# Loading q and k of six batches with the two heads of a pair side by side

## The chip, the core and the metric

The kernel runs on one core of one Trainium2 chip. The metric is device time in microseconds (us) of one execution, from launch to the last store. The core has five instruction queues that matter here: TensorE (PE; its weight loads are listed as PEld), VectorE (DVE), ScalarE (ACT), GpSimd (POOL) and SyncE (SP). Sixteen DMA engines move data between HBM and the on-chip memory; they serve the queues in which POOL, SP and ACT put their transfers.

## The reference

Eight batches of a 12-head attention with squared ReLU in the place of softmax, then a feed-forward layer over all 3584 tokens:

```python
# q, k, v: (batch 8, heads 12, seq 448, head_dim 64), float32
scale = 1.0 / np.sqrt(q.shape[-1])
scores = scale * np.matmul(q, k.transpose(0, 1, 3, 2))
attn = np.maximum(scores, 0.0) ** 2 / S          # S = 448
attn_out = np.matmul(attn, v)
# tokens side by side, heads joined: x is (3584, 768)
x = attn_out.transpose(0, 2, 1, 3).reshape(B * S, H * D)
h = x @ w_in                                     # w_in: (768, 2048)
g = 0.5 * h * (1.0 + erf(h * inv_sqrt2))         # exact GELU
return g @ w_out                                 # w_out: (2048, 768)
```

## The kernel before

**Stages.** Attention works on one batch `b` and one group `g` of four heads at a time (`G = 3` groups). The keys of a group are cut into seven blocks of 64 (`NK = 7`). A step (`add_steps`) is one block against all 448 queries for the four heads: TensorE makes the scores in 64-row tiles, two heads on the lower and two on the upper half of the partitions (L749); ACT or DVE scales them and takes the ReLU (L761, L763); DVE squares them (L770). After seven steps, `add_av` multiplies the squares by v (L810), and two copies bring the result to `xT`, the transposed input of the feed-forward layer. The first layer of that is plain for batches 0 to 4 (`add_f1`, L862, GELU in L872); for the last three batches it is cut in blocks and done with seven products in the place of eight on sums of the blocks (`add_wsums`, `add_blocks`, L1006, L1043), as is the second layer for all 14 groups of 256 tokens (`add_group`, L1179, L1213). All matmuls are bf16, and the loads of q, k, v and the weights convert from float32 on their way (POOL's queue).

**Transposed q and k.** The scores need q and k with the head dimension on the partitions (`qT`, `kT`). For batches 0 and 1 TensorE transposes them (`add_tk`, `add_tq`). For batches 2 to 7 a DMA of SP's queue does (`add_T_dma`, L660): it takes 128 columns of the loaded `nq` or `nk` at a time and lays them on 128 partitions. `nk` holds 7 column blocks of 64 for heads 0 and 1 of the group (one head on each half of the partitions), then 7 for heads 2 and 3; `nq` holds 4 column blocks for each of the four heads. The scores want heads 0 and 1 on the lower half of `qT` and `kT` and heads 2 and 3 on the upper, but a turned block of 128 columns has two blocks of the *same* head above each other (in the seventh of a group's k, one of each). The kernel before solves that in two ways. For k, the loop of the scores goes over the blocks in the order in which they lie, and the index of the square is worked out with `divmod` in `add_av`. For q, one turn per group fills every second slot of `qT` (`slots_of`), from a source that begins 64 columns into `nq` (which is two blocks of 64 longer, and zero in these), and `fill_halves` copies each half to the other half of the neighbouring slot: two copies for a group, by DVE or ACT. In `fn_qk` the moving operand is then picked by a slot number `n`.

**Order of the work.** The functions `add_...` only describe operations: which engines can do each and what it waits for. The list `ORDER` says which operation comes next on which engine: `P` is TensorE, `A` ACT, `D` DVE, `G` POOL, `S` SP, and the number is that of the operation in the order of creation; the class `Scheduler` merely places the operations by that list (`place`), and instructions run in that order on each engine. All gate and load numbers of POOL are in this list too.

**Loads.** POOL issues all loads. `nq` and `nk` have one buffer for all of batches 2 to 7, `qT` and `kT` have two. So loads of batch b+2 wait until batch b+1 is turned: a small POOL operation that reads `qT` of group g (`add_gate`, L709; `add_vgate`, L719) stands ahead of the loads of k and q of group g of the next batch (`add_k`, L546; `load_q`, L467) and holds POOL's queue until the turn has landed. A batch has three loads of k, three of q and one of v. POOL may have eight loads on the way; a load waits for the eighth before it. SP issues the turns (two per group, 36 in all) and the stores.

**Stores.** `store_rows` (L1140) writes 128 rows of the output. The row order of q within a batch is `(p c)` for all batches (query p x 4 + c stands in place c x 112 + p), so a tile of 128 rows is in two pieces of the output, and two DMAs store it; the last group uses SP and ACT for them.

**Buffers at the end.** `wtile` puts sums of `w_in` for the last three batches in buffers that q and k no longer need: `ws1` in that of `nq`, `ws4` in that of `nk`, `ws2` in one of the two of `qT`.

Of the kernel before, what the change touches and what calls it, by code (L numbers as in the profile page):

```python
# [13 lines left out]
KC = 112  # L14
# [10 lines left out]
SLOTS = H * NC + 1  # L25
# [58 lines left out]
A10 D13 G0 G1480 Z1024 P14 P11 D15 G1 G3 G4 G7 G118 G2 D12 A16 P17 P36 A37 G117 G121 G6 D18 P33 D34  # L84
P21 A22 P19 P39 A40 P42 G125 A43 P23 D20 D24 P51 A52 D35 P25 D26 P48 Z672 D41 D38 A49 G126 P63 A64
D50 P57 P66 A67 P31 P27 D32 P102 D65 A58 P108 D103 D28 D44 A109 P111 A112 D68 P29 D30 P54 A55 G5 D53
P69 P131 A70 D59 P45 D132 P96 A97 P90 A91 P129 P133 P81 P93 G8 G122 G120 D104 D46 A47 G124 A82 G119
D71 D134 D130 P72 G128 A94 P137 D56 D138 A73 D74 P75 D110 A76 P139 D83 P105 A106 D113 D107 D140 P60
A61 A62 P84 A85 P78 D98 P168 A79 A169 G123 G9 P141 P174 A175 G127 G239 G238 G241 G147 P114 A115 A116
D86 P162 D95 A163 P135 D92 P99 A100 A101 G148 D77 D80 P87 A88 P204 A89 D136 P198 A205 D170 A142 G150  # L90
D199 P145 A146 P165 D166 P171 D172 D173 P156 A157 D158 P243 A244 P247 A248 P183 G151 A184 P159 P207
D206 G153 G154 P257 D167 D164 A258 D160 D161 S228 S229 P255 A256 P253 A208 P189 A254 P213 A190 D176
P177 S231 D214 P180 A181 D178 P216 P267 D217 A179 G237 A268 P219 A220 D182 P195 S232 S234 P210 P249
D191 G240 D211 A250 D215 P265 A266 D196 D197 P143 P186 S235 P222 D221 G149 G152 G155 D218 A144 P192
D193 A223 P263 A264 P251 A187 D224 A252 P261 A262 P259 A260 D194 D188 D185 D200 P201 A202 D209 D212
P225 A226 D203 P245 A227 A246 P366 A367 P364 A365 P368 A369 P352 A353 D383 D384 P372 A373 P356 A357
D388 D380 D389 D381 D386 P378 A379 P348 A349 G242 G269 G270 G271 G272 D385 G273 G274 P354 A355 P370
D382 P362 A371 D387 P350 A363 A351 P360 D230 P285 A286 P291 A361 P288 A289 P374 A375 S408 P358 P294
D292 P282 A295 D293 A283 P276 P392 D233 P315 D287 D277 P318 D236 A359 D319 A316 P279 A280 A393 P376
P309 A310 P300 D317 A377 A301 D290 P333 P396 D278 D281 D284 D390 D296 D302 P394 D395 D311 S409 S411  # L100
S412 D391 A334 D335 P339 A340 P306 A307 P297 G417 A298 D299 D397 P327 A328 P398 P303 P324 G420 A325
D399 S414 S415 D429 D326 P312 A313 P400 D401 A304 D308 D314 D320 P402 D305 P404 D405 D427 D428 P330
A331 P336 D403 A337 D338 P321 D341 P342 A343 P431 P433 D410 A322 A323 P447 D432 A448 P459 A460 P453
D434 P435 A436 D454 D455 P450 A451 D413 P456 S406 A457 P462 D329 P437 P439 P471 G275 G423 G418 D344
A463 D332 P345 D438 A472 D440 G419 P477 P474 D430 A475 D570 D452 D458 P441 G421 A346 A347 D442 D449
A478 P443 D444 P480 D416 D461 P489 P465 A490 G422 G424 G425 A466 P539 A540 P525 A526 A481 P541 D464
S551 P486 A487 D467 A542 P507 D508 P468 P483 P504 A505 S407 S552 G560 A469 A470 S554 S555 D484 P521
A522 D473 P529 A530 G563 P513 P501 P495 D479 A496 S557 P545 A546 A514 D485 P543 A544 D476 S445 D509
# [50 lines left out]
A1395 A1355 P1425 D1424 A1375 D1426 P1427 D1428 A1389 P1429 A1361 D1433 D1434 P1437 A1438 D1430  # L159
D1435 P1439 D1440 S1431 S1432 D1436 P1441 D1442 P1443 D1444 P1445 D1446 P1447 D1455 P1449 D1448  # L160
D1453 D1454 P1457 D1450 D1456 P1459 D1458 D1460 P1461 P1463 D1462 S1451 S1452 S1473 D1464 P1465
D1466 P1467 D1468 P1470 S1474 P1469 D1471 D1472 S1475 S1476 S1477
"""


# [1355 lines left out]
```

## Time and profile before

| | |
|---|---|
| time, median of 3 runs (lowest to highest) | 365.88 us (365.56 to 365.89) |
| profiled execution: time, span | 365.83 us, 364.1 us |
| granted TensorE clock, mean over the span | 0.999 |
| loads of q in POOL's queue: number, KB, median us to landing | 21 of 224 KB, 8.7 |
| loads of k in POOL's queue | 23 of 224 KB, 8.2 |
| HBM read, written | 45.61 MB, 11.01 MB |

The span runs from the first to the last instruction of the trace; the time of an execution is 1.73 us more here. Times in the views below are in us from the start of the span, unless marked ns. A busy share says how long an engine had an instruction, not whether it was on the path that sets the end; that is read from the chain of waits, which goes back from the last instruction to what released each one. "issue" in such a place means that the engine waited for nothing that the profile shows. The DMA share is the mean busy share of 16 engines, and can go above 1 where it is added up over packets that overlap.

### The profile page before, as it was taken

The page shows a single profiled execution, that of the slowest core. Times are in us where ns is not written, and L with a number is a line of the kernel's source. Part 1 is how long each engine was busy: PE and PEld are TensorE (multiplying, and loading weights), DVE is VectorE, ACT ScalarE, POOL GpSimd, SP SyncE. Part 2 cuts the span into 40 slices and gives each one's busy share as a digit, 9 for nine tenths or more (in the row PEclk, how much of TensorE's full clock was granted, in tenths as well). Part 3 has the DMA queues.
Part 4 walks back from the last instruction along what each step waited for, and adds up shares of the span by engine and source line. Part 5 has one row for each costly group of instructions (what it writes and reads, how often), then busy time and mean ns, then how long its engine had stood idle before and what let it go on. Part 6 is the DMA issues. An engine that isn't in the chain of part 4 may idle for free.

```text
span 364.1 us, 8583 instructions
## 1 busy us (share of the span) xinstructions
PE 355.2 (98%) x3589; PEld 225.4 (62%) x3589; DVE 296.7 (82%) x515; ACT 214.3 (59%) x348; POOL 63.7 (17%) x104
## 2 busy tenths in 40 slices
PE   8889999999999999999999999999999999999995
PEld 3567555445555455454555556889888688867663
DVE  3988989299979998979989999999877775767662
ACT  4987755586777685888887887236353043214400
POOL 8565710431401404215010000000000000000000
PEclk9999999999999999999999999999999999999999
DMA  9999999999999999999795211002002030022223
GB/s 169 198 202 204 202 204 190 164 180 169 185 191 157 156 136 169 211 157 177 142 192 78 88 43 46 2 2 66 24 2 86 2 86 2 2 86 88 87 68 107
DMA packets 72326, 42.97 MB, mean 118 GB/s; under 512 B 37984, under 2 KB 68960, under 8 KB 72288
## 3 DMA queue, kind: packets, MB, share of 16 engines
q0 software_dynamic: 32912, 22.47, 43.9%
q1 hardware_dynamic: 38736, 19.46, 26.1%
q8 instruction: 28, 0.46, 0.5%
q10 hardware_dynamic: 640, 0.51, 0.4%
q14 instruction: 10, 0.08, 0.1%
HBM read 45.61 MB, written 11.01 MB: 156 GB/s over the span
## 4 chain that ended last, share of the span: by engine, by line
PE 90%; DVE 4%; DMA 3%; ACT 1%; issue 1%; DVEq 0%
PE pso L1179 34%; PE psh L862 21%; PE pb L1006 18%; PE ps L749 9%; PE pav L810 8%; DVE a_sq L770 2%; DMA out_dram<-osb 1%; ACT a_sq L761 1%; DMA k<-in_k_dram 1%; PE tp L605 1%; DVE a_sq L763 1%; DVE qT L511 1%; DVE osb L1213 0%; DVE kT L511 0%; DVE s_sb L1160 0%
## 5 line engine op out<-in xcount | busy, mean ns | idle before, releaser
L761 ACT ACTIVATE a_sq<-ps 128x896 bf16<-128x896 f32 (+1 forms) x137 | 120.0, 929 | 27.1 <-PE ps L749 26.8
L770 DVE TENSOR_TENSOR a_sq<-a_sq 128x896 bf16<-128x896 bf16 x169 | 96.9, 616 | 2.7 <-ACT a_sq L761 1.7
L862 PE MATMUL psh<-xT,win_sb 128*128 128x448 bf16 (+1 forms) x420 | 77.0, 337 | 0.0
L1179 PEld LDWEIGHTS <-s_sb 128*128 128x128 bf16 x456 | 43.0, 98 | 29.6 <-issue 4.9
L862 PEld LDWEIGHTS <-win_sb 128*128 128x128 bf16 x420 | 39.2, 98 | 35.3 <-issue 7.0
L1043 DVE TENSOR_TENSOR part<-pb,part 128x448 f32<-128x448 f32 x80 | 47.5, 620 | 16.5 <-PE pb L1006 15.4
L749 PE MATMUL ps<-qT,kT 64*64 64x448 bf16 (+1 forms) x756 | 49.1, 337 | 2.0 <-ACT a_sq L761 0.8
L1179 PEld LDWEIGHTS <-h_sb 128*128 128x128 bf16 x336 | 31.9, 98 | 22.6 <-issue 3.6
L872 ACT ACTIVATE h_sb<-psh 128x448 bf16<-128x448 f32 x64 | 35.2, 553 | 17.1 <-PE psh L862 16.9
L763 DVE TENSOR_SCALAR a_sq<-ps 128x896 bf16<-128x896 f32 x32 | 34.7, 1087 | 9.7 <-PE ps L749 9.4
L1179 PE MATMUL pso<-wout_sb,s_sb 128*128 128x384 bf16 (+2 forms) x232 | 41.1, 321 | 0.0
L1179 PE MATMUL pso<-wout_sb,h_sb 128*128 128x384 bf16 x224 | 41.1, 326 | 0.0
L1179 PE MATMUL pso<-t_sb,s_sb 128*128 128x384 bf16 x224 | 41.0, 326 | 0.0
L1006 PEld LDWEIGHTS <-win_sb 128*128 128x128 bf16 x384 | 36.8, 98 | 2.6 <-issue 0.4
L810 PE MATMUL pav<-a_sq,v_sb 64*64 64x448 bf16 (+1 forms) x756 | 36.2, 329 | 0.0
L749 PEld LDWEIGHTS <-kT 64*64 64x64 bf16 x756 | 19.2, 105 | 23.9 <-issue 18.1
L1213 DVE TENSOR_TENSOR osb<-pso,p_sb 128x384 f32<-128x384 f32 x42 | 23.2, 553 | 10.0 <-PE pso L1179 8.5
L1052 ACT ACTIVATE h_sb<-part 128x448 bf16<-128x448 f32 x48 | 24.4, 574 | 8.0 <-DVE part L1043 8.0
L1006 PEld LDWEIGHTS <-ws 128*128 128x128 bf16 x288 | 27.7, 98 | 1.7
L810 PEld LDWEIGHTS <-v_sb 64*64 64x64 bf16 x756 | 21.3, 107 | 10.8 <-issue 0.6
L513 ACT COPY part<-pb 128x448 f32<-128x448 f32 x16 | 8.1, 529 | 26.6 <-PE pb L1006 26.5
L513 ACT CAST xT<-pav 128x448 bf16<-128x448 f32 (+1 forms) x44 | 20.0, 501 | 5.0 <-PE pav L810 4.9
(61 smaller groups left out, 316.0 us busy)
## 6 DMA issues: line engine op xcount, KB each, us to landing
nk<-in_k_dram POOLq DMA_DIRECT2D x23, 224.0 KB, 8.2
nq<-in_q_dram POOLq DMA_DIRECT2D x21, 224.0 KB, 8.7
v_sb<-in_v_dram POOLq DMA_DIRECT2D x5, 672.0 KB, 8.2
out_dram<-osb SPq DMA_DIRECT2D x7, 336.0 KB, 4.1
v_sb<-in_v_dram POOLq DMA_DIRECT2D x9, 224.0 KB, 8.0
out_dram<-osb SPq DMA_DIRECT2D x7, 288.0 KB, 4.2
out_dram<-osb SPq DMA_DIRECT2D x8, 240.0 KB, 3.1
win_sb<-in_moe_w_in_dram POOLq DMA_DIRECT2D x8, 192.0 KB, 8.5
```

What stands on the lines that cost most here:

```text
L513: A.copy(dst, src)
L749: nc.tensor.matmul(ps[64 * j : 64 * j + 64, e, x * w : x * w + w], kT[r, g, i * 128 + 64 * j : i * 128 + 64 * j + 64], moving, start=True, ...
L761: A.activation(ar, ps, AF.Relu, scale=c_att)
L763: V.tensor_scalar(ar, ps, c_att, 0.0, op0=mybir.AluOpType.mult, op1=mybir.AluOpType.max,)
L770: V.tensor_mul(box["a2"][:, :, :used], ar, ar)
L810: nc.tensor.matmul(pav[0][o2 : o2 + 64, e, :w], vt[b][r, 2 * g + e, bass.ts(i, D)], box["a2"][r, y, o : o + w], start=(i == 0), stop=(i == ...
L862: nc.tensor.matmul(ph[:, x * n : x * n + n], win_sb[:, kd, bass.ts(m + x, 128)], xT[b][:, kd, c], start=(kd == 0), stop=(kd == KD - 1),)
L872: A.activation(h_ring()[:, m : m + nm, o + c.start : o + c.stop], box[0][:, :S].rearrange("p (x n) -> p x n", x=nm), AF.Gelu,)
L1006: nc.tensor.matmul(bank[name][:, y, z * HS : z * HS + HS], w[:, k, bass.ts(mm, 128)], right()[:, k], start=first and k == 0 and z == 0, st ...
L1043: V.tensor_add(get(to), ps(name), get(other))
L1052: A.activation(h_ring()[:, m : m + 2, o + half[c].start : o + half[c].stop], src().rearrange("p (x n) -> p x n", x=2), AF.Gelu,)
L1179: nc.tensor.matmul(box[bank][:, n0:n1], left()[:, kf], right()[:, kf, n0:n1], start=bool(need) and kf == 0, stop=kf == K2 - 1, skip_group_ ...
```

## The change

For batches 2 to 7, `nq` and `nk` are laid out with two heads beside each other: for each group, block after block, 64 columns of head 0 or 1 and 64 of head 2 or 3. A turned block of 128 columns then has one head on the lower 64 partitions and the other on the upper 64, as in batches 0 and 1. To lay them out so, a load of one group is cut in two DMAs (`e`), one for heads 0 and 1 and one for heads 2 and 3, whose pieces are 64 elements wide in the on-chip memory (128 B in bf16). The turns stay, one for k and one for q per group; the copies of `fill_halves` go, and so do the two memsets of the margins of `nq`. `fn_qk` and `add_av` use for all batches the indices that batches 0 and 1 had. `qT` is 112 columns shorter, and `ws2`, which lay in one of its buffers, gets a buffer of its own. The rows of q of batches 2 to 7 are in natural order, so a tile of 128 output rows from batch 2 on is one DMA; in the last group that means SP alone. `ORDER` is new as a whole: the order of the operations on TensorE, ACT, DVE, POOL and SP differs from about 14 us on (the numbers of the operations move as well, since 18 operations are gone).

```diff
-SLOTS = H * NC + 1
...
 ORDER = """
-A10 D13 G0 G1480 Z1024 P14 P11 D15 G1 G3 G4 G7 G118 G2 D12 A16 P17 P36 A37 G117 G121 G6 D18 P33 D34
+A10 D13 G0 G1462 Z1024 P14 P11 D15 G1 G3 G4 G7 G118 G2 D12 A16 P17 P36 A37 G117 G121 G6 D18 P33 D34
...
             elif b == 2:
-                nq[b] = natpool.tile([KC, (H * NC + 2) * D], BF16, tag="nq", name="nq")
-                nk[b] = natpool.tile([128, HP, NK * D], BF16, tag="nk", name="nk")
-                nc.gpsimd.memset(nq[b][:, :D], 0.0)
-                nc.gpsimd.memset(nq[b][:, D + H * NC * D :], 0.0)
+                nq[b] = natpool.tile([KC, G, 2 * NC, 2, D], BF16, tag="nq", name="nq")
+                nk[b] = natpool.tile([128, G, NK, 2, D], BF16, tag="nk", name="nk")
...
     def load_q(b, g0, g1, c0=0, c1=NC):
         get_nat(b)
-        nc.gpsimd.dma_start(
-            q_cols(b)[:, 4 * g0 : 4 * g1, c0 * D : c1 * D], q_view(b, g0, g1, c0, c1)
-        )
+        if b < 2:
+            to = nq[b][:, 4 * g0 : 4 * g1, c0 * D : c1 * D]
+            nc.gpsimd.dma_start(to, q_view(b, g0, g1, c0, c1))
+            return
+        for e in range(2):
+            h = 4 * g0 + 2 * e
+            rows = q[b, h : h + 2].rearrange("j (c p) d -> p (j c) d", p=KC)
+            nc.gpsimd.dma_start(nq[b][:, g0, :, e], rows)
...
-                tpool.tile([128, SLOTS * KC], BF16, tag="qT", name="qT"),
+                tpool.tile([128, HP * S], BF16, tag="qT", name="qT"),
...
     def add_k(b, g0, g1):
         def fn():
             get_nat(b)
-            nc.gpsimd.dma_start(nk[b][:, 2 * g0 : 2 * g1], kv_view(k, b, g0, g1))
-
-        o = dma(fn, (g1 - g0) * 4 * S * 256, war(b, g0, g1))
+            rows = kv_view(k, b, g0, g1)
+            if b < 2:
+                nc.gpsimd.dma_start(nk[b][:, 2 * g0 : 2 * g1], rows)
+                return
+            for e in range(2):
+                nc.gpsimd.dma_start(
+                    nk[b][:, g0, :, e], rows[:, e].rearrange("p (i d) -> p i d", d=D)
+                )
+
+        o = dma(fn, (g1 - g0) * 4 * S * 256, war(b, g0, g1), 1 + (b > 1))
...
-        o = dma(lambda: load_q(b, g0, g1, c0, c1), n, war(b, g0, g1))
+        o = dma(lambda: load_q(b, g0, g1, c0, c1), n, war(b, g0, g1), 1 + (b > 1))
...
-        def slots_of(n, o, k):
+        def q_dst(g):
             return lambda: get_T(b)[0].rearrange("p (s t) -> p s t", t=KC)[
-                :, 2 * n + o : 2 * (n + k) + o - 1 : 2
+                :, 2 * NC * g : 2 * NC * (g + 1)
             ]
 
-        def q_src(n, o, k):
-            return lambda: nq[b][:, 128 * n + D * o : 128 * (n + k) + D * o]
+        def q_src(g):
+            return lambda: nq[b][:, g].rearrange("p s e d -> p (s e d)")
...
         def k_src(g):
-            return lambda: nk[b][:, 2 * g : 2 * g + 2].rearrange("p e f -> p (e f)")
-
-        def fill_halves(g):
...
+            return lambda: nk[b][:, g].rearrange("p i e d -> p (i e d)")
...
-            even = turn(slots_of(8 * g, 1, 8), q_src(8 * g, 1, 8), lands)
-            both = sch.add(
-                (("DVE", 1.0, 1.1), ("ACT", 1.6, 1.7)), fill_halves(g), [even] + old_T(b)
-            )
-            for c, o in enumerate((even, both, both, both)):
-                Tq[b, g, c] = (o, o)
+            op = turn(q_dst(g), q_src(g), lands)
+            for c in range(NC):
+                Tq[b, g, c] = (op, op)
...
-            n = (16 * g + 15) * KC
-            nc.gpsimd.tensor_copy(gate, get_T(b)[0][:, n : n + 16])
+            n = 2 * S * (g + 1)
+            nc.gpsimd.tensor_copy(gate, get_T(b)[0][:, n - 16 : n])
...
-                            if b < 2:
-                                moving = q_rows(b)[r, 2 * g + j, cols(half)]
-                            else:
-                                n = 4 * (4 * g + 2 * ((2 * i + e) // NK) + j) + 1 - e
-                                moving = qT[r, n * KC : n * KC + S]
+                            moving = q_rows(b)[r, 2 * g + j, cols(half)]
...
-                        n, y = (i, e) if b < 2 else divmod(NK * e + i, 2)
-                        _, box, o = SQ[blocks[n]]
+                        _, box, o = SQ[blocks[i]]
...
-                            box["a2"][r, y, o : o + w],
+                            box["a2"][r, e, o : o + w],
...
-                part = tpool.tile([128, SLOTS * KC], BF16, tag="qT", name="ws2")
+                part = wpool.tile([128, 3 * h], BF16, tag="ws2", name="ws2")
...
         queue, j = list(queues or [nc.sync] * 2), 128 * t
+        if j >= 2 * S:
+            queue[-1].dma_start(out[j : j + 128, c], src[:, c])
+            return
         while j < 128 * t + 128:
```

More of the change, by code (lines that the diff above doesn't have):

```diff
@@ L158 @@
[L158 to L162 removed]
+D50 P57 P66 A67 P31 P27 D32 P102 D65 A58 P108 A109 D28 P29 A103 P131 D44 P45 P81 P69 A82 G5 G8 D68
@@ L716, in fn @@
         def fn(e):
-            nc.gpsimd.tensor_copy(gate, get_T(b)[0][:, 31 * KC : 31 * KC + 16])
+            nc.gpsimd.tensor_copy(gate, get_T(b)[0][:, 4 * S - 16 : 4 * S])
         pool_q.append(sch.add((("POOL", 0.2, 0.3),), fn, [Tq[b, 1, 0][0]]))
```

162 lines of the change are left out of this document (77 added, 85 removed).

## The prediction

> **What bounds the kernel now.** I read the page first: how full each engine is, and when.
>
> ```profile
> span 364.1 us, 8583 instructions
> PE 355.2 (98%) x3589; PEld 225.4 (62%) x3589; DVE 296.7 (82%) x515; ACT 214.3 (59%) x348; POOL 63.7 (17%) x104
> PE   8889999999999999999999999999999999999995
> DMA  9999999999999999999795211002002030022223
> q0 software_dynamic: 32912, 22.47, 43.9%
> ```
>
> TensorE is busy 98% of the span; in the first half of the span the DMA engines are never idle either. The table of stages says where TensorE is not busy (columns: stage, its length, then busy time of PE, PEld, DVE, ACT, POOL, granted clock, DMA share, GB/s):
>
> ```profile
> 6.00:32.00 26.00, 22.59 (x575) 16.57 (x572) 22.83 (x44) 22.96 (x37) 16.66 (x25) 1.00 1.34 198
> 32.00:200.00 168.00, 167.90 (x1613) 87.32 (x1614) 146.88 (x244) 124.64 (x188) 42.14 (x70) 1.00 1.14 171
> 200.00:340.00 140.00, 140.00 (x1267) 107.75 (x1264) 113.07 (x202) 63.54 (x120) 0.00 (x0) 1.00 0.14 41
> 340.00:364.10 24.10, 19.99 (x131) 12.24 (x129) 13.15 (x24) 0.69 (x2) 0.00 (x0) 0.98 0.35 99
> ```
>
> Between 32 and 340 us TensorE idles 0.1 us in 308. All slack that a change can win is the 3.4 us of idle time in 6 to 32 us (where ACT and DVE, 88% busy each, set the pace) and the 4.1 us of the tail. In the middle nothing can be won, but much can be lost: the scores of each batch need q and k loaded and turned in time, while DMA works at a share of 1.14. So the question is whether the new loads still arrive.
>
> **The change part by part.** *TensorE.* Both kernels issue the same 3589 matmuls in the same shapes. Four rows of the chain of waits price what the order moves (start, length, line, count):
>
> ```profile
> 74.14 1.41 PE pso L1179 x8
> 127.43 1.30 PE pso L1179 x8
> 114.00 6.92 PE psh L862 x36
> 89.84 1.32 PE pav L810 x28
> ```
>
> The first row is followed by scores in 64-row tiles, the second by other full products: the switch costs 0.11 us. The new order has one switch fewer. Gain 0.1 us.
>
> *The copies between halves* go, 36 of them:
>
> ```profile
> L511 DVE COPY qT<-qT 64x896 bf16<-64x896 bf16 x34 | 14.8, 436 | 4.1 <-DMA qT<-nq 3.3
> L513 ACT COPY qT<-qT 64x896 bf16<-64x896 bf16 x2 | 1.9, 937 | 0.0
> ```
>
> That is 14.8 us of DVE and 1.9 us of ACT, all after 66 us, beside a TensorE that never waits for them: worth the 0.1 us of idle time at most, taken as zero. Were TensorE not full there, a pair would cost 2 x 0.436 = 0.87 us between the landing of a turned q and its scores. That delay is gone, which I count below by comparing landings with scores directly.
>
> *The loads of q and k.* Before, k for four heads is 128 x 2 pieces of 896 B (as written) and q 112 x 4 pieces of 512 B. After, each is two DMAs and 1792 pieces of 128 B. No packet so small is in the trace. The nearest are four stretches, in this order: 8.5 to 9.5 us (all q pieces of 256 B), 13 to 14 us (896 B, with 15 completion words), 98.5 to 102.5 us (mixed loads of an attention batch), 137 to 139 us (transposes alone, 256 B each):
>
> ```profile
> DMA packets 660, 0.17 MB, mean 169 GB/s; under 512 B 660, under 2 KB 660, under 8 KB 660
> DMA packets 237, 0.20 MB, mean 199 GB/s; under 512 B 15, under 2 KB 237, under 8 KB 237
> DMA packets 1280, 0.80 MB, mean 199 GB/s; under 512 B 53, under 2 KB 1280, under 8 KB 1280
> DMA packets 2026, 0.50 MB, mean 251 GB/s; under 512 B 2026, under 2 KB 2026, under 8 KB 2026
> ```
>
> Per engine of 16: 16000/660 = 24.2 ns for 256 B and 16000/222 = 72.1 ns for 896 B, a line of 0.0747 ns/B. It gives 43.3 ns at 512 B. The mixed stretch fits: 64000/1227 = 52.2 ns at a mean of 652 B, line 53.8. Carried on to 128 B it gives 14.6 ns. The transposes, which read 256 B a packet as a new load piece does (f32), take 32000/2026 = 15.8. I take the mean of these two nearest rows, 15.2 ns. The far ends are 9.6 ns (bytes alone) and 24.2 ns (no cheaper than the smallest load packet seen).
>
> A batch's q and k cost 3 x (256 x 72.1 + 448 x 43.3)/16 = 7.1 us of each DMA engine before, and 3 x 3584 x 15.2/16 = 10.2 us after: d = +3.1 us per batch (2.7 at 14.6 ns, 3.5 at 15.8, 9.2 at 24.2, -0.6 at 9.6).
>
> The Trainium skill (DMA: Bandwidth & Descriptors, Specifications) asks 512 B or more for line rate and says that smaller transfers become read-modify-writes. The trace's 256 B packets show no such step; by the rule d would be the 9.2 of a rival below.
>
> *POOL's queue.* 36 issues more. Their time from the load of q:
>
> ```profile
> L467 POOL DMA_DIRECT2D nq<-in_q_dram x24: 727/742/980, 2.4 to 168.2; - x24
> ```
>
> 727 ns is a load of 448 pieces, 980 the one of 1344: 0.28 ns a piece, so 0.85 us for 896. Twelve take 10.2 us where six took 4.4. The pieces of one take 56 x 15.2 = 0.85 us of the engines: issue keeps up, nothing added. Each load also waits for the landing of the eighth before it, which binds only if eight such loads (6.8 us of work) land sooner than they are moved: zero. Two memsets of 0.17 us go. The gates and loads of v stay in place, behind later loads.
>
> *When loads must be there.* The gates on POOL run when a group's q is turned (below: the first q of batches 2, 3, 4 and 5, then the third of 5); the next loads are issued behind the last gate:
>
> ```profile
> 66.51 0.42 POOL L709 COPY gate<-qT 128x16 bf16<-128x16 bf16 x1 [12.77 <-DMA qT<-nq]
> 86.85 0.20 POOL L709 COPY gate<-qT 128x16 bf16<-128x16 bf16 x1 [10.50 <-DMA qT<-nq]
> 109.71 0.20 POOL L709 COPY gate<-qT 128x16 bf16<-128x16 bf16 x1 [13.64 <-DMA qT<-nq]
> 137.59 0.20 POOL L709 COPY gate<-qT 128x16 bf16<-128x16 bf16 x1 [11.12 <-DMA qT<-nq]
> 142.12 0.40 POOL L709 COPY gate<-qT 128x16 bf16<-128x16 bf16 x1 [1.50 <-DMA qT<-nq]
> ...
> 122.17 0.70 POOL L546 DMA_DIRECT2D nk<-in_k_dram  x1 [0.34 <-issue]
> 142.66 0.70 POOL L546 DMA_DIRECT2D nk<-in_k_dram  x1
> ```
>
> And the first scores of batches 2 to 7 on TensorE:
>
> ```profile
> 70.31 0.76 PE L749 MATMUL ps<-qT,kT 64*64 64x448 bf16 x12
> 93.99 0.95 PE L749 MATMUL ps<-qT,kT 64*64 64x448 bf16 x12
> 122.57 0.55 PE L749 MATMUL ps<-qT,kT 64*64 64x448 bf16 x8
> 150.80 0.55 PE L749 MATMUL ps<-qT,kT 64*64 64x448 bf16 x8
> 175.84 0.60 PE L749 MATMUL ps<-qT,kT 64*64 64x448 bf16 x8
> 199.67 0.36 PE L749 MATMUL ps<-qT,kT 64*64 64x448 bf16 x4
> ```
>
> The new TensorE order puts less or more before them: 8 matmuls of the second layer less (batch 3), 12 of the first less (4), one AV block less (5), 6 of the first more (6). By the four rows above that is -1.30, -12 x 0.192 = -2.3, -1.32 and +1.15 us. So the scores are wanted at 70.3, 92.7, 120.3, 149.5, 177.0 and 199.7. Loads of a batch go out only when the last q of the batch before is turned, so delays add up: the n-th batch from 2 is late by n x d against its gate. With d = 3.1: 69.6, 93.1, 119.0, 150.0. Batch 6 is today held by the scores of 4, not by its loads; a load phase of 137.59 - 122.17 = 15.4 us from 142.66 would end at 158.1, plus 5d = 173.6. Batch 7 follows at 158.1 + 4.5 (third q turned after the first) + 0.5 + 15.4 + 6d = 197.1. Batch 3 is late by 0.4 and batch 5 by 0.5. The delay is the largest of these, not the sum: +0.5 us. What is queued behind the waiting scores is all of TensorE's order, so it goes straight into the end. At d = 2.7 nothing is late.
>
> *SP's queue.* Turning itself keeps its 36 DMAs; stores of batches from 2 on are one DMA instead of two, 22 fewer. SP waits for its inputs anyway:
>
> ```profile
> SPq L660 <- DMA nk<-in_k_dram: 99.0, 6, 56.8
> ```
>
> So its shorter queue is worth zero.
>
> *Start and tail.* The order changes from about 14 us on. One gap stands out:
>
> ```profile
> 21.36 0.25 PE L605 MATMUL tp<-ident,nk 128*64 128x128 bf16 x2 [1.10 <-issue]
> ```
>
> It lies in the last turn of k of batch 1, which waited there for nothing that the profile shows; the new order has that turn 16 score matmuls later, and the gap may go (-1.1) or move. Against it, the first product now stands behind one score step more, that is one ReLU on one of two engines:
>
> ```profile
> L761 ACT ACTIVATE a_sq<-ps 128x896 bf16<-128x896 f32 (+1 forms) x137 | 120.0, 929 | 27.1 <-PE ps L749 26.8
> ```
>
> Half of 929 ns, +0.5. I take zero, ends -1.1 and +0.5. The last stores use SP alone, two of 128 rows, where SP and ACT shared them:
>
> ```profile
> 359.30 2.00 SPq L1140 DMA_DIRECT2D out_dram<-osb  x4
> 360.49 0.85 ACTq L1140 DMA_DIRECT2D out_dram<-osb  x2
> ```
>
> 0.5 or 0.43 us an issue, and both halves were issued at the same time: zero, +-0.3.
>
> Sum, against this execution's 365.83 us (the median of the runs is 365.88, 0.05 more): -0.1 + 0.5 = **366.2 us**.
>
> **The rivals.** *Loads starve the scores.* If the price in the crowded stage is 15.8 ns, batch 5 (the worst) is late by 137.59 + 4 x 3.54 - 149.48 = 2.3 us: 368.0. Past d = 2.9 the slope is steep, four to six us per us of d: at d = 5 batch 7 is late by 178.5 + 30 - 199.7 = 8.8: 374.5. For it: the DMA share is above 1 in this stage already. Against it: issue at 0.85 us keeps the load queue short, which lets turns pass sooner. *Each small piece moves its bytes twice*, 14.6 + 9.6 = 24.2 ns: batch 7 is late by 178.5 + 6 x 9.2 - 199.7 = 34 us: about 400. Against it: the 256 B packets lie on the line. (It is what the Trainium skill's rule, named above, would do here.) *The loads are hidden, and the start gains*: d at 2.7 or below and the gap of 1.10 us gone, 365.83 - 0.1 - 1.1 = 364.6, faster; it decides if the price is under 15 ns and no other gap opens. For it: at 14.6 ns every batch still has slack, 0.4 us at the least (batch 3). Against it: the same ACT and DVE work still paces the start.
>
> **How the numbers follow.** Just in time, as forecast: 0.46, own range 365.0 to 367.2. Starved: 0.28, middle 370. Double price: 0.06. Hidden with a gain at the start: 0.20. A measurement here tells about 0.2%, 0.73 us, from no change. Faster by that: 0.18 of the last case and 0.10 of the first, 0.28; within: 0.20 and 0.02, 0.22; slower: 0.16 + 0.28 + 0.06 = 0.50. The range runs from 364.4 (gain at the start, a little more) to 374.6 (d = 5), leaving out the double price and the outer parts of two cases.
>
> **What would show it.** Load packets of 128 B, about 84,000 in the load queue, some 3 us more load work per batch; gates of batches 2 to 5 at about 69.6, 93, 119, 150; no qT<-qT copies; TensorE idle between 32 and 200 us under 1 us, with any wait at the first scores of batches 3 and 5 and put down to the DMA of qT. A price under 14 ns, or loads whose waits overlap with turns, leaves no wait; more than 16 ns shows waits that grow from batch to batch. The start is right if the idle time of TensorE in 6 to 32 us stays near 3.4.

## The result: faster when the loads arrive, and they do not always

The changed kernel took 364.09 us in the median of four executions (363.45 to 364.39), the kernel before 365.86 (365.56 to 365.89): a ratio of 0.9954, 95% interval 0.9941 to 0.9966. That is 1.8 us less, where 366.2 was forecast, and 0.3 us below the range. Two later series of twelve executions each, on two chips, came out otherwise: medians of 366.07 (363.68 to 371.42; ratio 1.0015, 0.9985 to 1.0046) and 365.79 (363.72 to 369.25; ratio 1.0002, 0.9976 to 1.0028). The kernel before, in executions beside these, had medians of 365.4 and 365.6. In four of the series below the slowest execution (371.42, 369.25, 369.90 and 372.96 us) counts as slow; the ratios leave it out, and no conclusion rests on it. Both results have to be explained: a gain of 1.8 us, and its loss in about half of the later executions. Of these 24 only seven lie at or below 364.4, as all of the first four do; why the first four were all so fast stays open.

The page of the changed kernel, in an execution of 363.45 us:

```profile
span 361.6 us, 8548 instructions
PE 353.9 (98%) x3589; PEld 224.5 (62%) x3589; DVE 287.1 (79%) x487; ACT 209.2 (58%) x340; POOL 105.9 (29%) x138
PE   8889999999999999999999999999999999999995
DMA  9999999999999999999999711002001120202222
q0 software_dynamic: 85328, 22.47, 65.9%
```

The load queue has 85,328 packets for the same 22.47 MB, and its share of the engines grew from 43.9% to 65.9%. POOL's busy time went from 63.7 to 105.9 us. Yet TensorE's row looks as before. The stages (columns as in the prediction's table of stages):

```profile
6.00:32.00 26.00, 23.13 (x572) 17.04 (x570) 23.76 (x45) 24.01 (x38) 17.26 (x26) 1.00 1.36 200
32.00:200.00 168.00, 168.00 (x1619) 86.59 (x1618) 139.31 (x221) 120.21 (x184) 83.74 (x103) 1.00 1.62 167
200.00:340.00 140.00, 140.00 (x1259) 108.14 (x1258) 110.85 (x198) 62.47 (x116) 0.00 (x0) 1.00 0.14 46
340.00:361.60 21.60, 17.96 (x119) 11.01 (x117) 12.30 (x23) 0.00 (x0) 0.00 (x0) 1.00 0.29 108
```

By busy time TensorE gained 0.1 us between 32 and 200 us. That reading is wrong, and the forecast rested on it. A matmul that is pipelined counts as busy to its modelled end: one of the scores is listed with 0.35 us, though the next step can follow 0.19 us after its start. So most of a wait of 0.3 us between two steps of scores vanishes under it. So I counted otherwise: each matmul gets the time by which matmuls of its kind follow each other when nothing is in the way (0.189 us for 448 columns, in proportion for others; four 64-row tiles side by side count as one), and at a given amount of finished work the time lost so far is the clock minus that sum. The changes between tile sizes are in it; the changed kernel has one fewer, worth 0.1 us by the prediction's rows. Time lost in each stage, from the starts of all 3589 matmuls, in us (the stages end at the work that the kernel before has finished at 13 and at 31 us):

| profiled execution | up to 13 us (same code) | 13 to 31 us | 31 us to the last matmul's start | from there to the end of the span |
|---|---|---|---|---|
| before | 4.99 | 3.79 | 13.26 | 4.34 |
| changed | 4.45 | 3.20 | 12.36 | 3.89 |
| changed, third series | 5.04 | 3.40 | 14.35 | 3.89 |

The span is 2.5 us shorter: 0.5 ahead of any change, 0.6 in the start, 0.9 in the middle, 0.4 to 0.5 in the tail. The 0.5 ahead of the change is one execution against another. The chain of waits shows it at the first transposes, of before and then of the changed kernel (start, length, line, count):

```profile
5.81 0.43 PE tp L605 x8
```

```profile
5.24 0.43 PE tp L607 x8
```

Other executions of either kernel began between these two or later. This is most of why 2.5 us of span are 1.8 us of medians.

Where the 0.9 us of the middle was hidden, the order in time of before shows (start, length, engine, line). Twelve matmuls of three score steps take 0.76 us when nothing is late:

```profile
145.26 0.76 PE L749 MATMUL ps<-qT,kT 64*64 64x448 bf16 x12
152.69 1.06 PE L749 MATMUL ps<-qT,kT 64*64 64x448 bf16 x12
...
152.03 1.08 DVE L763 TENSOR_SCALAR a_sq<-ps 128x896 bf16<-128x896 f32 x1
```

The second step at 152.69 needed the buffer of an earlier step, whose ReLU DVE began only at 152.03 and ended 0.4 us after the scores had begun. The prediction itself quotes such a row, 0.95 us for twelve at 93.99, and did not read it; there the trace names one of the copies in `qT` as what came last. Before, 20 of 24 such groups take 0.76 or 0.77 us and four take 0.90, 0.95, 0.96 and 1.06, some 0.8 us too much in all; in the changed kernel all 21 that stand in one row take 0.76. The Trainium skill (Perfetto Trace Analysis, Identifying the Most-Contended Engine) says that matmul occupancy is no good measure of how close TensorE is to its limit, because matmuls are pipelined. This trace agrees: 0.1 us of idle time, and some 0.8 us of waits in four groups of the same stretch.

### The profile page after: what moved, and what is told of

Same layout as the page of the kernel before. It is cut to its first block, busy times and chain, and to the rows that moved or that the text cites. A ratio compares the mean times of both kernels' runs of the same rounds, so it can differ in the third digit from the quotient of the medians.

```text
span 361.6 us, 8548 instructions
## 1 busy us (share of the span) xinstructions
PE 353.9 (98%) x3589; PEld 224.5 (62%) x3589; DVE 287.1 (79%) x487; ACT 209.2 (58%) x340; POOL 105.9 (29%) x138
## 3 DMA queue, kind: packets, MB, share of 16 engines
q0 software_dynamic: 85328, 22.47, 65.9%
## 4 chain that ended last, share of the span: by engine, by line
PE 94%; ACT 4%; DMA 1%; DVE 0%; issue 0%; DVEq 0%
PE pso L1164 36%; PE psh L844 21%; PE pb L988 18%; PE ps L732 10%; PE pav L792 9%; ACT a_sq L744 3%; DMA k<-in_k_dram 1%; PE tp L607 0%; PE tp L635 0%; ACT xT L508 0%; DVE nk L506 0%; DVE kT L506 0%; DVE osb L1198 0%; ACT qT L508 0%; DVEq L1501 0%
## 5 line engine op out<-in xcount | busy, mean ns | idle before, releaser
L744 ACT ACTIVATE a_sq<-ps 128x896 bf16<-128x896 f32 (+1 forms) x132 | 115.0, 923 | 26.0 <-PE ps L732 25.6
L746 DVE TENSOR_SCALAR a_sq<-ps 128x896 bf16<-128x896 f32 x37 | 40.3, 1088 | 13.0 <-PE ps L732 12.8
L732 PE MATMUL ps<-qT,kT 64*64 64x448 bf16 (+1 forms) x756 | 47.7, 336 | 1.5 <-ACT a_sq L744 0.7
L1034 ACT ACTIVATE h_sb<-part 128x448 bf16<-128x448 f32 x48 | 25.5, 577 | 26.8 <-DVE part L1025 26.8
L546 POOL DMA_DIRECT2D nk<-in_k_dram x36 | 34.7, 968 | 9.0 <-DMA wout_sb<-in_moe_w_out_dram 7.8
L732 PEld LDWEIGHTS <-kT 64*64 64x64 bf16 x756 | 18.3, 105 | 22.7 <-issue 17.0
L464 POOL DMA_DIRECT2D nq<-in_q_dram x36 | 30.0, 837 | 2.3 <-DMA wout_sb<-in_moe_w_out_dram 2.1
```

The costliest lines, as they stand in the source:

```text
L464: nc.gpsimd.dma_start(nq[b][:, g0, :, e], rows)
L546: nc.gpsimd.dma_start(nk[b][:, g0, :, e], rows[:, e].rearrange("p (i d) -> p i d", d=D))
L732: nc.tensor.matmul(ps[64 * j : 64 * j + 64, e, x * w : x * w + w], kT[r, g, i * 128 + 64 * j : i * 128 + 64 * j + 64], moving, start=True, ...
L744: A.activation(ar, ps, AF.Relu, scale=c_att)
L746: V.tensor_scalar(ar, ps, c_att, 0.0, op0=mybir.AluOpType.mult, op1=mybir.AluOpType.max,)
```

## The experiments

### The parts one by one, and old and new crossed

**Old order for the new data.** The changed kernel with the old `ORDER`, the 18 copy operations left out of it and the numbers moved up:

```diff
-D50 P57 P66 A67 P31 P27 D32 P102 D65 A58 P108 A109 D28 P29 A103 P131 D44 P45 P81 P69 A82 G5 G8 D68
+D50 P57 P66 A67 P31 P27 D32 P102 D65 A58 P108 D103 D28 D44 A109 P111 A112 D68 P29 D30 P54 A55 G5 D53
...
```

> The changed kernel with the order of operations of the kernel before (the 18 copy operations left out of it, nothing else moved). Theory H (TensorE did wait before, in the third step of groups of three score steps, for ReLUs and copies that DVE had late; four such groups were 0.14 to 0.29 us too long, some 0.9 us in all in the middle of the kernel): without the copies at least the 0.18 us wait on a copy at 94.1 us goes, at most the 0.9, and the single stores of the tail give 0.4: 364.6 to 365.3 us. Theory O (the new order alone brings the gain, data layout nothing but the tail): 365.4. Theory L (small pieces cost time and the order hides that): slower than before, above 366.

366.30 us (364.19 to 369.90), ratio 1.0011, 0.9988 to 1.0035: no gain, and eleven of twelve executions between 364.19 and 369.24. In its trace TensorE idled 0.68 us for the third turned q of batch 5, and then 1.97 us behind a store: a product waited for an addition of DVE, and that for a buffer that a store had not yet freed (idle time before, and what ended it):

```profile
156.67 1.14 PE L1164 MATMUL pso<-t_sb,h_sb 128*128 128x384 bf16 x6 [1.97 <-DVE osb L1198]
...
156.06 0.56 DVE L1198 TENSOR_TENSOR osb<-pso,p_sb 128x384 f32<-128x384 f32 x1 [3.51 <-DMA out_dram<-osb]
```

So with the small pieces in the old order there is no gain, and turned q and stores come late. Theory L is nearest, but its "slower than before" isn't shown: the interval holds 1. Theory H names only part of what happens. That the new order makes room for the small pieces isn't shown either: the later series of the changed kernel (below) lie as near to the kernel before (ratios 1.0015 and 1.0002) and spread as widely, in the new order.

**New order for the old data.** The kernel before in the new order, each pair of copies put in by hand:

```diff
-D50 P57 P66 A67 P31 P27 D32 P102 D65 A58 P108 D103 D28 D44 A109 P111 A112 D68 P29 D30 P54 A55 G5 D53
+D50 P57 P66 A67 P31 P27 D32 P102 D65 A58 P108 A109 D28 P29 A103 P131 D44 P45 P81 P69 A82 G5 G8 D68
...
```

> The kernel before, with its large load pieces, its copies and its two-piece stores, in the order of the changed kernel; each pair of copies is put as many operations ahead of its first scores as before. Theory H: the start gains 0.5 us, the tail nothing, the middle between 0 and 0.5: 364.9 to 365.4. Theory O: all but the tail's 0.4 comes with the order: 364.5. If the old layout needs the old order (copies late where the new order wants q sooner): 366 or more, with waits on copies.

382.2 us (381.4 to 383.6), beyond all but the last expectation, and far beyond what that had in mind. By the count above it loses 18 us more than the kernel before between 31 us and the last matmul. The trace shows 11.9 us of TensorE's idle time there: 2.9 for copies in `qT`, 2.1 for ReLUs of ACT and DVE, 3.1 for nothing that the profile shows, the rest for other work of ACT and DVE. The new order gives DVE five more ReLUs (37 for 32), and the copies' 14.3 us come on top; that this is why DVE comes late is argued, not shown. Where I put the copies is arbitrary, so this shows only that the new order does not suit the old layout with the copies in these places.

**No copies, all else old.**

```diff
-                :, 2 * n + o : 2 * (n + k) + o - 1 : 2
+                :, 2 * n + 8 : 2 * n + 16
...
-                copy(e, t[:64, n + 2 : n + 17 : 2], t[64:, n + 1 : n + 16 : 2])
-                copy(e, t[64:, n : n + 15 : 2], t[:64, n + 1 : n + 16 : 2])
+                return
...
-                                n = 4 * (4 * g + 2 * ((2 * i + e) // NK) + j) + 1 - e
+                                n = 16 * g + 8 + 4 * j
```

> The kernel before, order and loads unchanged, but the copies between halves are not made; a turn of q fills eight slots beside each other and the scores read these, so they take wrong columns of q. Theory H: faster by 0.2 to 0.9 us, 365.0 to 365.7, and the long score groups at 77.4, 84.4, 94.0 and 152.7 us shrink, the one at 94.0 for certain. As predicted (copies lie beside a TensorE that never waits): 365.86, no change.

365.42 us against 365.61, ratio 0.9998, 0.9989 to 1.0006: between 0.4 us faster and 0.2 slower. Its groups at 77, 84 and 94 us take 0.76; but two later executions that kept the copies were free of these three waits too, so that the copies made them isn't shown. In the profiled execution a new wait stood in their place: DVE waited 3.21 us for a store, which landed 0.2 us after a load of v that POOL had issued ahead of it, and TensorE then idled 0.41 us for DVE.

**New start.** The first 287 operations of the new list, up to about 33 us, then the old one:

```diff
-D50 P57 P66 A67 P31 P27 D32 P102 D65 A58 P108 D103 D28 D44 A109 P111 A112 D68 P29 D30 P54 A55 G5 D53
+D50 P57 P66 A67 P31 P27 D32 P102 D65 A58 P108 A109 D28 P29 A103 P131 D44 P45 P81 P69 A82 G5 G8 D68
...
```

> The kernel before, with the changed kernel's order for the first 287 operations of the list (all that runs up to about 33 us), then its own order for the rest. If the new order of the start is worth what the two traces show between 13 and 31 us (0.4 to 0.6 us less idle time of TensorE): 365.1 to 365.4, against 365.6 to 365.9 for the kernel before. If that difference was only one execution against another: no change. If a gain of the start is lost again where TensorE waits for loads anyway: no change, but a start as in the changed kernel and longer waits behind it.

365.15 against 365.41, ratio 0.9994, 0.9986 to 1.0003. In its trace the start (13 to 31 us) loses 3.19 us, as in the changed kernel (3.20), where before loses 3.79; the median moved by 0.3. So the order of the start is worth something like 0.3 to 0.6, at the edge of what can be measured.

**One store for 128 rows, last group only.**

```diff
+        if t >= 2 * NG - 2:
+            queue[-1].dma_start(out[j : j + 128, c], src[:, c])
+            return
```

> The kernel before, but its last group stores each 128 rows (or the part of the columns that is ready) with one DMA of SP's queue in the place of two pieces on SP and ACT; these rows come out in another order. If the shorter tail of the changed kernel is due to that: 0.4 us faster, 365.2 to 365.5, and 0.4 us less between the last matmul and the end of the span. As predicted (worth zero, within 0.3): 365.6 to 365.9.

364.82 against 365.41, ratio 0.9978, 0.9969 to 0.9987: 0.6 us, shown. From the start of the last matmul to the end of the span it takes 3.7 us where before takes 4.3. Before, four DMAs store the last two parts; the later of each queue is issued at 360.89 and 360.96, 1.2 us after that start, and lands 1.9 us on. Now two do, both on SP; the later is issued 1.15 us after the last matmul's start, hardly sooner, and lands 1.6 us on. So 0.3 us is gained between issue and landing, and 0.2 behind the last landing; why fewer stores land sooner isn't shown.

**These three at once**, the three edits above in one kernel, loads and the order from 33 us on still old:

> The kernel before with three parts of the change at once: no copies (the scores read other columns of q), the new order up to about 33 us, and the last group stored by single DMAs of SP. Its loads are the old large ones, and its order from 33 us on is the old one. Alone the three parts gave 0.2, 0.3 and 0.6 us. If they add up and the new order of the middle is worth the rest: 1.0 to 1.1 us faster than the kernel before, and slower than the changed kernel by 0.6 to 0.8. If the three are the whole gain (the rest was one part hiding another): as fast as the changed kernel, 1.6 to 1.9 us faster than before.

364.40 (363.90 to 365.19), ratio 0.9973, 0.9965 to 0.9982: 1.0 us, about what the three gave alone (0.2, 0.3 and 0.6). They add up, within what can be measured.

### Do the small pieces cost anything?

**Large pieces in the changed kernel**, two series on two chips:

```diff
-        for e in range(2):
-            h = 4 * g0 + 2 * e
-            rows = q[b, h : h + 2].rearrange("j (c p) d -> p (j c) d", p=KC)
-            nc.gpsimd.dma_start(nq[b][:, g0, :, e], rows)
+        to = nq[b][:, g0].rearrange("p s e d -> p (s e d)").rearrange("p (h f) -> p h f", h=4)
+        nc.gpsimd.dma_start(to, q_view(b, g0, g1, c0, c1))
...
+            to = nk[b][:, g0].rearrange("p i e d -> p (i e d)")
+            nc.gpsimd.dma_start(to.rearrange("p (x f) -> p x f", x=2), rows)
...
```

> The changed kernel, but q and k of batches 2 to 7 are loaded as before, one DMA per group in pieces of 512 and 896 B as written, into the same bytes (so the heads lie in the wrong columns). If the small pieces are wholly hidden: 364.1, within 0.3. If they still cost something (POOL's issue of 0.9 us each, later turns): faster than 363.8. If the larger pieces crowd the turns: slower than 364.4.

> The changed kernel with the old large load pieces (heads in the wrong columns), again, on the same chip as the changed kernel itself. Its slack was 3.9 to 8.5 us where that of the changed kernel was 1.0 to 3.4. Theory E: all executions within 1 us, median 363.6 to 364.1, whatever the changed kernel does beside it. Rival C, or a spread that comes from the new order alone: as wide as the changed kernel.

363.85 (363.60 to 364.10; ratio 0.9956, 0.9944 to 0.9968) and 364.11 (363.60 to 364.62; 0.9956, 0.9941 to 0.9971). The first series, beside the first four executions of the changed kernel, looked as if the small pieces were wholly hidden. The second stood on one chip with the changed kernel:

> The changed kernel once more, beside the two kernels below on the same chip, and for a second profile of it. The gain read from the two traces at hand is 2.5 us of span, of which 0.5 us lies ahead of the first matmul that differs (one execution against another); so some 1.8 us less than the kernel before in the median, and in the middle (32 to 225 us) again no wait of TensorE beyond its changes between tile sizes.

> The changed kernel a third time, as the base for the two below on one chip. Its executions so far lay at 363.5 to 364.4 and, on another chip, at 363.7 to 371.4. Theory E (edge): its loads have 1 to 2.5 us of slack, and an execution in which the DMA engines slow down for some us loses more; so again a spread of more than 2 us, and the profiled execution's time above 364 is explained by waits of the scores for turned q or by stores that land late. Rival C (the chip of the second series was at fault): a spread below 1 us here, around 364.

366.07 and 365.79, as told above; the 1.8 us less that the first of the two expected did not come. With large pieces the same order gives nine executions within 1.0 us; with small ones, on the same chip, eleven of twelve lie between 363.72, as fast as with large ones, and 368.78. So rival C falls, and so does the new order alone: the way of loading causes the spread. Piece size and the second DMA per group go together in this edit; which of the two it is, it does not say. The trace of the third series shows how (order in time; the row at 143.14 has the wait):

```profile
139.84 1.50 PE L792 MATMUL pav<-a_sq,v_sb 64*64 64x448 bf16 x28
143.14 0.57 PE L732 MATMUL ps<-qT,kT 64*64 64x448 bf16 x8 [1.80 <-DMA qT<-nq]
```

These are the first scores of batch 5. In the execution of 363.45 us they ran at 140.38. The wait is most of the 2.0 us that this trace loses more in the middle. How much room there is, taken from the landing of the first turned q of each batch and the start of its first scores (us; 0.1 is what a wait leaves):

| batch | 2 | 3 | 4 | 5 | 6 | 7 |
|---|---|---|---|---|---|---|
| before | 3.9 | 7.3 | 11.5 | 8.2 | 14.2 | 14.0 |
| changed, 363.45 us | 1.0 | 2.5 | 3.3 | 1.9 | 1.5 | 4.2 |
| changed, third series, 366.44 us | 1.7 | 1.1 | 2.0 | 0.0 | 0.1 | 4.3 |
| changed, large pieces | 3.9 | 5.9 | 8.1 | 5.2 | 8.5 | 12.5 |

What eats the room differs from execution to execution. The load of v of batch 4 and the third turn of that batch run together, and in that stretch the DMA engines now and then nearly stand still. Four microseconds out of it, in before (from 113 us), in the changed kernel's first trace (from 120) and in its second series (from 120):

```profile
DMA packets 1031, 0.52 MB, mean 130 GB/s; under 512 B 814, under 2 KB 975, under 8 KB 1031
```

```profile
DMA packets 847, 0.98 MB, mean 244 GB/s; under 512 B 62, under 2 KB 722, under 8 KB 847
```

```profile
DMA packets 423, 0.24 MB, mean 59 GB/s; under 512 B 214, under 2 KB 422, under 8 KB 423
```

The third turn lands after it, the gate behind that turn holds all loads of batch 5, and these then need some 15 us until the first q is turned. The kernel before has the slow stretch too, and 8 us of room to take it. What slows the engines there stays open.

**A delay by hand** ahead of the loads of batches 3 to 7, four memsets (2.95 us) and one (0.74):

```diff
+            if b > 2 and g0 == 0:
+                for _ in range(4):
+                    nc.gpsimd.memset(delay, 0.0)
...
+    delay = const.tile([128, 768], BF16, tag="delay", name="delay")
```

> The changed kernel with four memsets on POOL ahead of the loads of each of batches 3 to 7, some 3 us in all per batch by the plan: the delay that the prediction put on the small pieces, made by hand. If the delays add up from batch to batch and the changed kernel has only 1 to 2 us of slack left: first waits at the scores of batch 4 or 5, 367 to 376. If the loads have slack of more than the sum, or POOL waits in that time anyway: within 0.3 us of the changed kernel, 364.1.

> The changed kernel with one memset of 0.74 us on POOL ahead of the loads of each of batches 3 to 7 (a quarter of the delay that cost 6.2 us). Slack between the landing of the first turned q and its first score was 2.5, 3.3, 1.9, 1.5 and 4.2 us for batches 3 to 7. If the delay adds up from batch to batch (0.7, 1.5, 2.2, 3.0, 3.7): late by 0.3 us at batch 5 and 1.5 at batch 6, 1 to 3 us slower than the changed kernel. If each batch takes up its delay in its own slack: within 0.3 us of the changed kernel.

370.33 (369.82 to 370.95) and 369.76 (366.90 to 372.96). The first is what the forecast's rival of starving loads said: idle times of 1.89 and 1.02 us ahead of scores of batches 3 and 4, and 5 us over the kernel before. The second can't be told from the spread: in its trace TensorE never idles for turned q, but 2.7 us where a product waits for a buffer that a store holds. That a quarter of the delay cost nearly as much as all of it fits neither of its theories.

**Pieces of 64 B for k:**

```diff
+                to = nk[b][:, g0].rearrange("p i x (e d) -> p (i x) e d", e=2)
                 nc.gpsimd.dma_start(
-                    nk[b][:, g0, :, e], rows[:, e].rearrange("p (i d) -> p i d", d=D)
+                    to[:, :, e], rows[:, e].rearrange("p (i d) -> p i d", d=D // 2)
```

> The changed kernel with the pieces of k of batches 2 to 7 cut to 64 B (so twice as many, the same bytes; the columns of two heads change places in blocks of 32). By the straight line through the 256 B and 896 B packets a piece of 64 B costs 9.8 ns and one of 128 B 14.6: 3 x 1792 x (2 x 9.8 - 14.6)/16 = 1.7 us more load work per batch. If a piece has a floor near that of 128 B: 4.5 us more or above. Then turns are later by that and more from batch to batch, and the time tells how near the edge the loads are: 364.1 if there is slack for it, 366 to 372 if not.

377.33 us (376.1 to 379.3), waits at every batch from 2 to 5, and more than the 366 to 372 expected without slack; why so much more isn't settled. The price of a piece, from 2 us of the changed kernel (152 to 154) with 128 B pieces alone and 1 us of this one (109 to 110) with 64 B alone:

```profile
DMA packets 2434, 0.31 MB, mean 153 GB/s; under 512 B 2434, under 2 KB 2434, under 8 KB 2434
```

```profile
DMA packets 1835, 0.12 MB, mean 125 GB/s; under 512 B 1825, under 2 KB 1835, under 8 KB 1835
```

32000/2434 = 13.1 ns of an engine for 128 B, 16000/1835 = 8.7 for 64 B. The line through 256 and 896 B gave 14.6 and 9.8. That the 256 B packets lie on this line, as the prediction argued against a step, is no evidence, since it was drawn through them; the two new sizes are. No step shows at any of these sizes; the read-modify-write that the Trainium skill (DMA: Bandwidth & Descriptors, Specifications) gives for transfers under 512 B would show as one, and the measurement decides.

### A version with room

POOL's queue holds all loads of a batch behind the third gate, and v ahead of it. Here k and q of each group go out behind their own gate, and v later; nothing else changes (shown for the loads of batch 6):

```diff
-P610 A611 P613 D639 P565 D511 D512 P567 A614 G559 D566 D568 P628 P634 D612 A635 D636 G711 P640 P569
+P610 A611 P613 D639 P565 D511 D512 P567 A614 G559 D566 D568 P628 P634 D612 A635 D636 G711 G712 G713
...
-A590 D657 A650 S710 P827 D828 D651 A647 A648 P591 P785 G714 G560 P658 S579 P664 A665 P593 G717 G712
-A659 G713 G715 G716 G718 A786 D592 P595 D663 D666 D594 D660 P779 P761 A762 D780 P670 A671 A672 P764
+D654 P646 A590 D657 A650 S710 P827 D828 D651 A647 A648 P591 P785 G714 G715 G716 P658 S579 P664 A665
+P593 G717 G560 A659 G718 A786 D592 P595 D663 D666 D594 D660 P779 P761 A762 D780 P670 A671 A672 P764
```

G711, G714 and G717 are gates, G560 the load of v; the others load k and q. The same is done for the loads of batches 4, 5 and 7, in batch 4 with v one gate sooner.

> The changed kernel, complete, with only POOL's queue in another order for the loads of batches 4 to 7: k and q of a group go out right behind the gate of that group, and the load of v (672 KB, of the batch before) behind the third gate (for v of batch 3 behind the second), where the changed kernel has gate, gate, v, gate and then all loads of k and q. First loads of batches 4 to 7 go out 5 to 10 us sooner; v lands 4 to 5 us later than now, where it has 8 to 13 us. Theory E: slack of the first q of batches 5 and 6 grows from 1 to 2 us to 4 or more, the spread falls below 1.5 us, median 363.5 to 364.2, and no wait of scores for turned q. If the loads of the next batch slow the third turn and v more than they gain: as wide as the changed kernel, or slower.

364.62 us (364.09 to 366.99), ratio to before 0.9974, 0.9957 to 0.9992, beside 365.79 for the changed kernel on the same chip. Ten of twelve executions are within 0.9 us. The first turned q, by the gates of batches 4 and 5, comes earlier by 2 and 5 us than in the fastest trace of the changed kernel:

```profile
111.90 0.20 POOL L696 COPY gate<-qT 128x16 bf16<-128x16 bf16 x1 [4.93 <-DMA qT<-nq]
133.75 0.20 POOL L696 COPY gate<-qT 128x16 bf16<-128x16 bf16 x1 [2.98 <-DMA qT<-nq]
```

Theory E holds in part: with the same small pieces and more room ten of twelve executions lie at or below 364.92, where nine of twelve of the changed kernel lie at 365.26 or above. But the spread is 2.9 us, not below 1.5, and the median is above the 363.5 to 364.2 that it gave. The room at batch 6 was still 2.1 us, not 4, and in the profiled execution (365.82) TensorE idled 0.95 us in the way told above, at a store that freed its buffer late. It is faster than both kernels as they stand, by 1.0 us over before and 0.8 to 1.2 over the changed one on that chip (without and with its slowest execution).

## Why the prediction was wrong

- *TensorE never waits in the middle.* This step failed. "Between 32 and 340 us TensorE idles 0.1 us in 308" took the busy share for the absence of waits. From 31 us to the last matmul three executions in the old order with copies lost 12.7 to 13.3 us, and three of the new order without late loads 12.3 to 12.4: 0.4 to 0.9 us, most of it in score groups. So "nothing can be won" was false, and the zero for the copies and the rest of the order stood on it. What of the 0.9 is due to the copies and what to the order isn't settled: without copies alone 0.2 us, not clear of zero, and the old order lost as much without them (12.7 and 12.9). Where the forecast's sum has -0.1 + 0.5, the first result has about -0.3 to -0.6 at the start, -0.4 to -0.9 in the middle, -0.4 to -0.6 in the tail and no wait.
- *The wait of +0.5 at batch 5.* The forecast's two terms were both wrong and happened to meet. Its wanted times for batches 4 to 7 came from the wrong rows: the first scores of a batch are issued among the last ones of the batch before, at 121.06, 145.66, 174.11 and 194.95, not at 122.57, 150.80, 175.84 and 199.67; the changed kernel wanted those of batch 5 at 140.4, not 149.5. And the delay does not add up as n x d with d = 3.1:

```profile
68.44 0.20 POOL L696 COPY gate<-qT 128x16 bf16<-128x16 bf16 x1 [7.51 <-DMA qT<-nq]
88.87 0.20 POOL L696 COPY gate<-qT 128x16 bf16<-128x16 bf16 x1 [4.98 <-DMA qT<-nq]
113.66 0.38 POOL L696 COPY gate<-qT 128x16 bf16<-128x16 bf16 x1 [7.40 <-DMA qT<-nq]
138.61 0.20 POOL L696 COPY gate<-qT 128x16 bf16<-128x16 bf16 x1 [4.11 <-DMA qT<-nq]
```

  Forecast were 69.6, 93.1, 119.0 and 150.0. Against the same order with large pieces the first q of batches 2 to 7 landed 2.3, 2.9, 4.2, 2.8, 6.5 and 7.8 us later: some 1.1 us more per batch after the first. The price of 13.1 ns gives 1.7 (3 x 3584 x 13.1/16 - 7.1); I had chosen 15.2, the mean of the line's 14.6 and the transposes' 15.8.
- *Loads starve the scores*, chance 0.28, was right in what happens (scores wait for turned q, in the later series at batch 5), and its edge was real: some executions fall over it and most others come within 1 to 3 us of it. Its condition was not: it asked for 15.8 ns a piece, and at the measured 13.1 the prediction said that no wait would be left. The waits come with a deadline of batch 5 that is 9 us earlier than it took it to be, and with the slow stretches of the DMA engines, neither of which it had. The forecast gave one time where the kernel has a spread; a "just in time" with 0.4 us of margin should have said so.
- *Start*, zero with ends -1.1 and +0.5: about -0.3 to -0.6 by trace and experiment. The gap of 1.10 us is gone; idle times of 0.38, 0.16 and 0.32 stand behind 20 us instead. The sign was open and the size inside the ends. The profile's 0.5 us ahead of the change is no part of it.
- *Tail*, zero +-0.3: -0.6 by the experiment, outside its own ends, so this term failed too. Its reading of the issue held: the last store goes out only 0.02 to 0.09 us sooner. Left out was the time from issue to landing, which it took to be the same: 1.6 us with two stores, 1.9 with four.
- *What held:* 85,328 load packets for some 84,000; an issue of 0.84 to 0.97 us for 0.85; no `qT<-qT` copies; SP's shorter queue is nowhere on the path; the rival of bytes moved twice (about 400 us) did not come. The switch (-0.1) was not measured on its own.
- *Rivals.* The four executions of the result are the rival "hidden, and the start gains" (364.6, chance 0.20), with two more gains that it did not have (tail and middle), so that its nearness in time is partly luck; the later series lie at 365.8 to 366.1, in the forecast's own range, but by gains and waits that cancel and not by its sum.

## What to carry to other kernels

A TensorE that is busy 99.9% can still wait: compare the lengths of like groups of matmuls (0.76 against 0.95 or 1.06 us for twelve), or count finished work against the clock. A transfer that is just in time makes a kernel whose time varies; give its room in microseconds for each deadline, beside how much a slow stretch of the DMA engines takes (here 2 to 4 us: the third turn of batch 4 landed at 123.1, 124.9 and 127.1 us in three executions of one kernel), and measure more than four executions. Where a queue of loads waits behind one gate, look for the loads that need only an earlier gate.

## What the runs showed of the hardware

A wait of TensorE can cost more than its length. Behind 1.89 us of idle time (the kernel with four memsets, up to 97.1 us) and behind 1.97 us (new data in the old order, up to 156.7) the granted clock was halved for 3.41 us (98.35 to 101.76 us, and 157.97 to 161.38); behind the 1.80 us of the third series it stayed full. The stretches behind the wait, in this order (columns as before, the granted clock third from the end):

```profile
97.00:101.00 4.00, 3.87 (x24) 1.94 (x25) 2.16 (x3) 1.73 (x2) 3.28 (x6) 0.67 0.95 192
```

```profile
156.60:161.50 4.90, 4.83 (x48) 2.40 (x51) 4.78 (x9) 0.92 (x1) 4.18 (x6) 0.65 2.38 158
```

```profile
143.10:147.10 4.00, 3.96 (x36) 1.83 (x39) 3.49 (x6) 2.53 (x3) 0.20 (x1) 1.00 1.84 187
```

Half the clock for 3.41 us is a loss of another 1.7 us, nearly the wait again. The length of the wait does not decide it alone: in the kernel with 64 B pieces the clock stayed full behind 2.67 us of idle time (up to 95.3 us), and in the old data with the new order it fell 1 us after the end of an idle time of 1.68 us (up to 96.7). One such stretch takes 0.005 off the mean granted clock of an execution (0.5 x 3.41/365, an estimate). In the two later series of the changed kernel, the slowest execution of each left out, four of 22 have a mean of 0.994 or 0.995, and they are four of the five slowest, from 367.83 us on; the others have 0.998 or more. So the clock is part of the spread; the rest would be the waits themselves, which only a profiled execution shows. The Trainium skill (TensorE: Matmul & The Clock Gate, Part 1) puts the drop after an idle window of about 3.4 us that runs freely; here idle times of 1.68 to 1.97 us were enough in three traces.
